# Buffers taken in turn instead of first-free in a one-core attention and mixture kernel

## The chip, the cores and the metric

The kernel runs on one core of a Trainium2 chip. The metric is device time in microseconds (us), the median of several executions. TensorE (PE) does the matmuls; its weight loads have a row of their own (PEld). VectorE (DVE), ScalarE (ACT) and GpSimd (POOL) do the elementwise work, SyncE (SP) issues the transfers. Each engine works through its own list of instructions in order, and waits on semaphores for the others. PSUM, into which the matmuls write, has eight banks of 128 partitions by 512 float32 values.

## The reference, cut to what matters

Two layers follow each other. In the first, each of 4 x 8 heads has 768 queries and keys of 64 values; a query attends only to keys in the same of 64 buckets, which the signs of six projections give. The second is a mixture of 4 causal attention experts over the 512 joined values, of which each position takes the best two.

```python
q_bits = (np.einsum('bhsd,dk->bhsk', q, proj) > 0)          # k_bits alike
mask = q_bucket[:, :, :, None] == k_bucket[:, :, None, :]
scores = np.where(mask, scale * np.matmul(q, k.transpose(0, 1, 3, 2)), -1e9)
x = softmax(scores) @ v                                      # per head, then joined to (B, S, 512)
...
logits = x @ w_gate                                          # the best 2 of 4 experts, softmax weights
for e in range(E):
    scores = np.where(causal, -1e9, scale * (x @ wq[e]) @ (x @ wk[e]).transpose(0, 2, 1))
    out += weight_of(e) * (softmax(scores) @ (x @ wv[e]) @ wo[e])
```

## The kernel before

The program first records its operations, then issues them in a fixed order that is stored in the file (`ORDER`). For each operation the stored order also says on which engine it runs, where two were offered. `Recorder.issue` walks through that order. When an operation touches a tile for the first time, `issue` allocates it from its pool under its name, with `bufs` buffers for that name (`c.pool.tile(...)`), and then calls the engine's method. That call is line 183, and so nearly all instructions of the profile carry line 183; they are told apart by the tiles that they write and read. The order of the instructions on every engine is the order of this list.

The work is a pipeline over units: 32 units "L" (a head of the first layer) and 16 units "M" (an expert of the second, for one batch). Each unit takes these steps, and the steps of several units run beside each other:

- Preparation. For the first layer `prep_pair` does two heads at once. Four times it has ScalarE scale a window of q or k into a PSUM bank named `mx` (`mx<-natq,cs`, `mx<-natk,cs`), copies that to float16 (`qk<-mx` on ScalarE or VectorE) and has VectorE subtract the copy to get the low half (`qk<-mx,qk`). Then 12 small matmuls into `misc` give the bucket signs (`misc<-qk,pbh`). For experts `proj_steps` makes the `qk` tiles from matmuls into `misc`.
- Row maxima. `max_steps` does matmuls into banks named `mx` (`mx<-qk`), and VectorE reduces each to maxima (`pm<-mx`, or `scrap<-mx,causal` in the masked form). `shift_steps` turns the maxima round through `misc` into a row (`negh`, `row`, `fr`) that is added to the queries by a transfer.
- Scores. `s_unit` does matmuls into banks named `st` (`st<-qk`). ScalarE takes the exponential twice, in float32 (`p<-st`) and float16 (`ph<-st`), and GpSimd subtracts (`pl<-p,ph`), so that the attention weights stand in two float16 halves.
- Values. Three matmuls for each 128 keys go into the bank `o` (`o<-vh,ph`, `o<-vl,ph`, `o<-vh,pl`), four or five chunks behind the scores; VectorE divides by the sum (`xp<-o,rden`, `yn<-o,rden`).

The eight PSUM banks are shared out by name: `misc` has two, `o` one, `mx` two, `st` three. The two `mx` banks so serve the ScalarE windows of `prep_pair` and the max matmuls of `max_steps` together:

```python
w = psum.tile([128, 512], FT, name="mx", bufs=2)[:, 0:HS]       # prep_pair
nc.scalar.activation(w, x, AF.Copy, scale=cn)
nc.copy(a[:, ev], w)
marks["t"] = nc.vector.tensor_tensor(r, w, a[:, ev], op=OP.subtract)
...
p = psum.tile([128, 512], FT, name="mx", bufs=2)                # max_steps
nc.tensor.matmul(p[:, o:o + w], d["qa"][0:kr, qs], d["ka"][0:kr, k0:k1], start=True, stop=True)
```

Of the names in SBUF with several buffers, `qk` has 12, `xt` 8, `ph` 7, `pl` 5, `p32` 4, `xp` and `xs` 3, and `fr`, `row`, `rden`, `ot`, `yn`, `wst`, the loads `natq`, `natk`, `natv` and some small ones 2. Where a tile takes a buffer that another tile had, its first operation waits until all operations on the earlier tile are done. In the kernel before, the allocation itself picks the buffer: of the buffers of a name, the one that was given up first, as the program's build reckons it.

Of the kernel before, what the change touches and what calls it, by code (L numbers as in the profile page):

```python
# [115 lines left out]
class Recorder:  # L116
# [56 lines left out]
    def issue(self):  # L173
        def real(x):
            if not isinstance(x, View):
                return x
            return x.real()

        for o, (e, m, args, kw) in self.schedule():
            for c in o.new:  # L180
                if c.real is None:
                    c.real = c.pool.tile(c.shape, c.dtype, name=c.name, bufs=c.bufs)
            getattr(getattr(self.nc, e), m)(*[real(x) for x in args], **{k: real(x) for k, x in kw.items()})  # L183


# [1280 lines left out]
```

## Time and profile before

| | us |
|---|---|
| median of 3 runs | 612.49 (612.16 to 612.70) |
| profiled execution | 612.32 |
| its span, first to last instruction | 610.5 |
| TensorE busy | 591.4 |
| VectorE busy | 524.0 |
| ScalarE busy | 516.8 |
| GpSimd busy | 471.5 |

The granted clock of TensorE was 1.000 of full speed. The busy time of an engine is the part of the span that its instructions cover; matmuls overlap each other, and their ends are modelled, so a TensorE that is busy is not one at its peak. In a timeline an instruction has its start, its duration, its operation as out<-in, and in square brackets how long its engine had been idle and what released it.

### The profile page before, as it was taken

Reading aid. Unit: us, or ns where it says so; the run is one execution under the profiler, and the core shown is the slowest. Engines: PE = TensorE matmul, PEld = TensorE weight load, DVE = VectorE, ACT = ScalarE, POOL = GpSimd, SP = SyncE. Lnnn points to the kernel's source line nnn. Section 1 sums busy time; section 2 is a strip of 40 time slices with the busy share of each in tenths; the row PEclk is TensorE's granted clock in tenths of the full one; section 3 lists DMA queues with packets and bytes.
Section 4 is the critical chain, followed back from the end, with each engine's and each line's share of the span. In section 5 each row is a group of like instructions: output and inputs, shape, how many; then the busy total and the mean of one; then the engine's idle time right before and its main releaser. Section 6 shows DMA issues by size and latency. Waiting matters only on the chain.

```text
span 610.5 us, 20339 instructions
## 1 busy us (share of the span) xinstructions
PE 591.4 (97%) x7754; PEld 432.8 (71%) x7754; DVE 524.0 (86%) x1440; ACT 516.8 (85%) x1132; POOL 471.5 (77%) x540
## 2 busy tenths in 40 slices
PE   8999999999999999999999999999899999999996
PEld 4788887777676767776667676777666677767663
DVE  6999999898899999888989998978988978557973
ACT  7989999999889899958869999987977988934774
POOL 8899989977687889768777888976856888942661
PEclk9999999999999999999999999999999999999999
DMA  6666352231512122331333143222222121001322
GB/s 188 169 189 195 81 146 68 56 99 48 153 40 58 41 87 61 102 104 32 92 89 87 37 119 101 58 83 73 68 87 75 45 48 42 16 21 28 87 79 104
DMA packets 36313, 51.22 MB, mean 84 GB/s; under 512 B 8212, under 2 KB 26104, under 8 KB 36216
## 3 DMA queue, kind: packets, MB, share of 16 engines
q1 hardware_dynamic: 36056, 49.93, 29.7%
q8 instruction: 61, 1.00, 0.7%
q14 instruction: 36, 0.29, 0.2%
q10 hardware_dynamic: 160, 0.00, 0.0%
HBM read 20.98 MB, written 6.29 MB: 45 GB/s over the span
## 4 chain that ended last, share of the span: by engine, by line
PE 67%; DVE 17%; ACT 8%; issue 3%; POOL 2%; DMA 2%; SPq 1%; DVEq 0%; ACTq 0%; POOLq 0%
PE misc L183 22%; PE st L183 19%; PE o L183 16%; PE mx L183 10%; DVE pm L183 6%; ACT p L183 3%; ACT ph L183 3%; DVE qk L183 2%; DVE xt L183 1%; DVE misc L183 1%; POOL pl L183 1%; DVE pmw L183 1%; DMA natq<-in_q_dram 1%; SPq L183 1%; ACT xt L183 1%
## 5 line engine op out<-in xcount | busy, mean ns | idle before, releaser
L183 POOL TENSOR_TENSOR pl<-p,ph 128x512 f16<-128x512 f32 x370 | 409.4, 1126 | 111.3 <-ACT p L183 32.4
L183 PE MATMUL st<-qk 128*128 128x512 f16 (+12 forms) x928 | 229.7, 325 | 2.1 <-ACT p L183 1.0
L183 ACT ACTIVATE ph<-st 128x512 f16<-128x512 f32 x372 | 214.0, 609 | 15.2 <-PE st L183 11.1
L183 ACT ACTIVATE p<-st 128x512 f32<-128x512 f32 x372 | 215.9, 609 | 11.7 <-PE st L183 8.9
L183 PEld LDWEIGHTS <-ph 128*128 128x128 f16 x2880 | 168.1, 98 | 35.5 <-issue 6.5
L183 DVE TENSOR_REDUCE pm<-mx 128x2 f32<-128x512 f32 (+1 forms) x248 | 162.9, 673 | 11.2 <-PE mx L183 8.3
L183 PEld LDWEIGHTS <-pl 128*128 128x128 f16 x1440 | 133.3, 97 | 16.8 <-issue 4.1
L183 PEld LDWEIGHTS <-qk 128*128 128x128 f16 (+4 forms) x1248 | 109.1, 98 | 46.9 <-issue 9.2
L183 PE MATMUL mx<-qk 76*128 76x512 f16 (+2 forms) x464 | 134.3, 326 | 7.2 <-DVE qk L183 4.5
L183 PE MATMUL o<-vh,ph 128*128 128x65 f16 (+1 forms) x1104 | 138.8, 194 | 0.3 <-DVE xp L183 0.3
L183 PE MATMUL o<-vh,pl 128*128 128x65 f16 (+1 forms) x1104 | 138.8, 193 | 0.3 <-POOL pl L183 0.3
L183 PE MATMUL o<-vl,ph 128*128 128x64 f16 x1104 | 138.1, 192 | 0.0
L183 PE MATMUL misc<-xt,wqk_h 128*128 128x384 f16 x256 | 58.6, 325 | 0.0
L183 DVE CUSTOM_DVE_ANT_0 scrap<-mx,causal 128x512 bf16<-128x512 f32 (+2 forms) x96 | 44.4, 462 | 8.8 <-PE mx L183 7.0
L183 DVE TENSOR_REDUCE pmw<-mx 128x2 f32<-128x512 f32 x68 | 44.9, 681 | 2.3 <-PE mx L183 2.0
L183 PE MATMUL o<-mvh,pl 128*128 128x65 f16 x336 | 40.6, 193 | 0.6 <-DVE yn L183 0.6
L183 PE MATMUL o<-mvl,ph 128*128 128x64 f16 x336 | 40.9, 192 | 0.0
L183 PE MATMUL o<-mvh,ph 128*128 128x65 f16 x336 | 40.6, 193 | 0.1
L183 POOL TENSOR_TENSOR vl<-vf,vh 128x384 f16<-128x384 f32 x32 | 29.5, 928 | 11.1 <-PE misc L183 5.1
L183 PEld LDWEIGHTS <-xt 128*128 128x128 f16 x324 | 29.6, 97 | 10.7 <-issue 1.8
L183 PEld LDWEIGHTS <-wqk_h 128*128 128x128 f16 x256 | 24.0, 97 | 14.5 <-issue 1.6
L183 PE MATMUL misc<-wvg_h,xt 128*128 128x260 f16 x192 | 32.1, 274 | 0.7 <-ACT row L183 0.7
(226 smaller groups left out, 1001.2 us busy)
## 6 DMA issues: line engine op xcount, KB each, us to landing
qk<-qk SPq DMA_DIRECT2D x128, 96.0 KB
natv<-in_v_dram SPq DMA_DIRECT2D x16, 384.0 KB
natq<-in_q_dram SPq DMA_DIRECT2D x15, 384.0 KB
natk<-in_k_dram SPq DMA_DIRECT2D x15, 384.0 KB
out_dram<-ot SPq DMA_DIRECT2D x20, 256.0 KB
qk<-qk SPq DMA_DIRECT2D x96, 48.0 KB
qk<-qk SPq DMA_DIRECT2D x8, 192.0 KB
qk<-M SPq DMA_DIRECT2D x48, 24.0 KB
```

What stands on the lines that cost most here:

```text
L183: getattr(getattr(self.nc, e), m)(*[real(x) for x in args], **{k: real(x) for k, x in kw.items()})
```

## The change

A counter is kept for each pool and name. A tile of a name with several buffers is now allocated under that name with a number behind it, which goes round from 0 to `bufs` - 1, and each of these numbered names has a single buffer. So the buffers of a name are used in turn, in the order in which the operations are issued. The list of operations, the engines on which they run and the number of buffers of each name stay as they are.

```diff
+        turn = {}
         for o, (e, m, args, kw) in self.schedule():
             for c in o.new:
                 if c.real is None:
-                    c.real = c.pool.tile(c.shape, c.dtype, name=c.name, bufs=c.bufs)
+                    k = turn[c.pool, c.name] = turn.get((c.pool, c.name), -1) + 1
+                    c.real = c.pool.tile(c.shape, c.dtype, name=f"{c.name}{k % c.bufs}" if c.bufs > 1 else c.name, bufs=1)
             getattr(getattr(self.nc, e), m)(*[real(x) for x in args], **{k: real(x) for k, x in kw.items()})
```

## Rows read from the trace of the kernel before

**Rows 1.** The page: busy time of TensorE, and the chain's shares by engine.
```profile
PE 591.4 (97%) x7754; PEld 432.8 (71%) x7754; DVE 524.0 (86%) x1440; ACT 516.8 (85%) x1132; POOL 471.5 (77%) x540
...
PE 67%; DVE 17%; ACT 8%; issue 3%; POOL 2%; DMA 2%; SPq 1%; DVEq 0%; ACTq 0%; POOLq 0%
```

**Rows 2.** Waits over the span: who waited for whom, us, times, longest.
```profile
DVE pm L183 <- PE mx L183: 8.3, 14, 1.7
...
PE mx L183 <- DVE qk L183: 4.5, 10, 0.9
...
PE st L183 <- ACT p L183: 1.0, 2, 0.6
...
PE st L183 <- ACT ph L183: 0.5, 2, 0.3
```

**Rows 3.** Busy time of each engine by stretch (first column: the stretch).
```profile
core 0: us, PE busy (x) PEld busy (x) DVE busy (x) ACT busy (x) POOL busy (x), PEclk, DMA share, GB/s
108.00:115.00 7.00, 6.83 (x88) 5.33 (x86) 5.12 (x18) 7.00 (x16) 7.00 (x7) 1.00 0.05 10
...
220.00:223.00 3.00, 2.74 (x31) 1.77 (x28) 2.90 (x10) 3.00 (x8) 2.31 (x2) 1.00 0.21 49
288.00:298.00 10.00, 9.01 (x137) 6.40 (x135) 9.42 (x29) 10.00 (x23) 8.56 (x10) 1.00 0.24 71
...
298.00:364.00 66.00, 65.70 (x872) 45.43 (x870) 60.39 (x161) 56.64 (x125) 50.83 (x49) 1.00 0.31 86
...
396.00:402.00 6.00, 5.40 (x61) 4.22 (x58) 4.62 (x17) 5.97 (x15) 3.33 (x4) 1.00 0.06 15
433.00:443.00 10.00, 7.91 (x130) 5.66 (x129) 8.59 (x28) 8.94 (x21) 8.40 (x9) 1.00 0.13 33
```

**Rows 4.** Timeline of TensorE, 435 to 442 us.
```profile
435.25 0.38 PE L183 MATMUL mx<-qk 65*128 65x512 f16 x1 [0.48 <-DVE qk L183]
...
435.83 0.19 PE L183 MATMUL o<-mvh,ph 128*128 128x65 f16 x1
435.86 0.19 PE L183 MATMUL o<-mvl,ph 128*128 128x64 f16 x1
...
438.18 0.39 PE L183 MATMUL mx<-qk 65*128 65x512 f16 x1 [0.91 <-DVE qk L183]
...
441.25 0.27 PE L183 MATMUL mx<-qk 65*128 65x256 f16 x1 [0.70 <-DVE qk L183]
```

**Rows 5.** Timeline of ScalarE, 437 to 440 us.
```profile
437.31 0.27 ACT L183 ACTIVATE fr<-misc 12x128 f16<-12x128 f32 x1 [0.37 <-PE misc L183]
...
438.73 0.56 ACT L183 ACTIVATE mx<-natk,cs 128x384 f32<-128x384 f32 x1
439.96 0.60 ACT L183 ACTIVATE ph<-st 128x512 f16<-128x512 f32 x1 [0.67 <-PE st L183]
```

**Rows 6.** Timeline of VectorE, 435 to 439 us.
```profile
435.78 0.69 DVE L183 CUSTOM_DVE_ANT_0 scrap<-mx,causal 128x512 bf16<-128x512 f32 x1 [0.31 <-PE mx L183]
...
437.58 0.55 DVE L183 TENSOR_TENSOR qk<-mx,qk 128x384 f16<-128x384 f32 x1
438.61 0.69 DVE L183 TENSOR_REDUCE pm<-mx 128x1 f32<-128x512 f32 x1 [0.48 <-PE mx L183]
```

**Rows 7.** Timelines of ScalarE (windows) and VectorE (subtractions) at three other places.
```profile
146.14 0.66 ACT L183 ACTIVATE mx<-natk,cs 128x384 f32<-128x384 f32 x1
...
296.19 0.67 ACT L183 ACTIVATE mx<-natk,cs 128x384 f32<-128x384 f32 x1
...
366.53 0.72 ACT L183 ACTIVATE mx<-natk,cs 128x384 f32<-128x384 f32 x1
...
145.91 0.55 DVE L183 TENSOR_TENSOR qk<-mx,qk 128x384 f16<-128x384 f32 x1
...
296.15 0.56 DVE L183 TENSOR_TENSOR qk<-mx,qk 128x384 f16<-128x384 f32 x1
...
365.89 0.54 DVE L183 TENSOR_TENSOR qk<-mx,qk 128x384 f16<-128x384 f32 x1
```

## The prediction

> **What bounds the kernel now.** I read the busy shares and the chain that ended last first. TensorE is busy 97% of the span, and 67% of the chain is its own work; VectorE holds 17% of it, ScalarE 8% [rows 1]. So time is won only where TensorE stands still, or where VectorE or ScalarE stands on the chain. Second, the waits. TensorE waits for nothing much: the largest entry that buffers can explain is "PE mx <- DVE qk", 4.5 us in 10 waits [rows 2]. A matmul that writes a fresh `mx` bank waits until a VectorE subtraction that writes `qk` is done. No data goes that way: the max matmul reads `qk` tiles of another unit, and what the subtraction does with an `mx` bank is to read and free it. It is a wait for a buffer, which is exactly what the change deals with. Third, the stretches in which these waits lie [rows 3]: 2.1 of the 4.5 us fall into 433 to 443 us (0.48, 0.91 and 0.70, [rows 4]), the rest, 2.4 us, in seven single waits of 0.2 to 0.6 us in 108 to 115, 144 to 148, 188 to 194, 220 to 223, 288 to 298, 364 to 370 and 396 to 402 us. They are the places where `prep_pair` runs beside the max matmuls of a mixture unit.
>
> Look at one of them. At 438.18 the max matmul starts, 0.05 us after the subtraction of 437.58 (0.55 us long) ends, having stood 0.91 us [rows 4, 6]. There are two `mx` banks. The other was given up by the `scrap<-mx` operation that began at 435.78 and took 0.69 us, so at 436.47 [rows 6]. It then lay idle until ScalarE wrote the next `prep_pair` window into it at 438.73 [rows 5]. The bank that was free went to the engine that came late, and the engine that came early was sent to the bank in use.
>
> **What the change does, part by part.** It adds no instruction, removes none and reorders none. Each tile gets buffer number (its count modulo the number of buffers), so it waits for the tile that many places before it in the list of operations, where before it waited for the one whose buffer the allocation had listed as free first. I followed that list for each name. For `p32`, `ph`, `pl`, `pf`, `row`, `rden`, `xp`, the `nat` tiles, `wst`, `yth`, `ytl` and `yn` the tiles are given up in the order in which they are taken, so nothing changes. Another predecessor comes to 50 of 432 `mx` tiles in PSUM, 60 of 240 `misc`, 6 of 393 `st`, 69 of 96 `qk`, 6 of 30 `xt`, 4 of 20 `ot` and 2 of 31 `fr`. Mostly two neighbours in the list swap buffers.
>
> *Removed: the `mx` waits behind `prep_pair`.* In the list the ScalarE window of `prep_pair` stands just ahead of the max matmul, so in turn the window gets the bank of the subtraction and the matmul the bank that is free. In the example the matmul's new predecessor is done at 436.47, 1.71 us before the matmul starts [rows 4, 6]; all ten places are of this kind. The gross gain is the 4.5 us of rows 2. It can be more: a matmul's end is modelled, and 65-column matmuls of 0.19 us start every 0.03 us [rows 4], so each idle time may be up to 0.16 us longer than shown. Ten of these make 1.6, and the upper bound is 6.1 us.
>
> How much is kept? In 433 to 443 us ScalarE is busy 8.94 of 10.00 us and VectorE 8.59, so neither is full [rows 3], and both stand still because of these waits: VectorE 0.31 and 0.48 us for the max matmul itself [rows 6], ScalarE 0.67 us for the next `st` matmul, and 0.37 us for a `misc` one [rows 5]. ScalarE's two make 1.04, which is the least that this stretch gives back; 2.1 is the most. I take 1.5. Elsewhere ScalarE is full: 7.00 of 7, 3.00 of 3, 10.00 of 10, 5.97 of 6 us [rows 3]. There TensorE gets ahead, and whether the lead lasts hangs on what it meets next. After such a stretch TensorE is the pacer again (65.70 of 66 us busy, ScalarE 56.64), and it has to wait for an `st` bank only 1.0 and 0.5 us in the whole run [rows 2, 3], so some lead can be carried out. Between nothing and 2.4 us I take the middle and a little, 1.3.
>
> *Added: the ScalarE window waits for the subtraction.* In most places ScalarE comes to it later than the subtraction ends: at 366.53 the window starts 0.10 us after the subtraction of 365.89 (0.54 us) [rows 7]. In two it would be clearly late: at 296.19 its new predecessor ends at 296.15 + 0.56 = 296.71, 0.52 us later, and at 146.14 it ends at 145.91 + 0.55 = 146.46, 0.32 us later [rows 7]. What stands behind the window on ScalarE are the exponentials of the attention unit, for which GpSimd and then the value matmuls wait. If ScalarE passes all of it on it costs 0.84 us; nothing, if the subtraction itself moves up by what VectorE no longer waits. I take 0.4.
>
> *`misc`, `st`, `xt`, `qk`, `ot`, `fr`.* These swaps I cost at nothing. `misc`, `st` and `xt` swap neighbours both of which are long free, or late by less than 0.2 us. `qk` has 12 buffers and its predecessors are units that ended tens of microseconds before. What hides a single late `qk` tile near 112 us is VectorE's idle time, busy 5.12 of 7.00 us [rows 3]; uncovered it costs at most one VectorE operation of 0.55 us.
>
> *The sum:* 1.5 + 1.3 - 0.4 = 2.4 us. The profiled execution took 612.32 us with a span of 610.5, and lies 0.17 us under the median of 612.49. So 612.32 - 2.4 = 609.9 for that execution and 610.1 for the median.
>
> **Rivals.** *ScalarE holds the gain (no change).* Outside 433 to 443 us ScalarE is full wherever TensorE waits [rows 3], so the lead of TensorE is used up at the next exponential, and in 433 to 443 us only ScalarE's 1.04 us comes back, less the 0.84 us of late windows: 0.2 us, 612.3. For it speak the rows with 10.00 of 10; against it that TensorE hardly ever waits for an `st` bank [rows 2], and that ScalarE is not full after the stretches. The Trainium skill says the same in general: "Perfetto Trace Analysis", section "Identifying the Most-Contended Engine", has the engine with the highest occupancy be the one to improve, and warns that matmul busy time doesn't tell how near TensorE is to its limit. By that rule the 97% of TensorE prove nothing, ScalarE is the engine that counts in these stretches, and the time stays where it is; the trace agrees within the stretches, and not between them.
>
> *All of it is kept.* If TensorE paces everything, 4.5 us go and the hidden parts with them, up to 6.1, with no cost: 606.2 to 607.8 us.
>
> *Slower: ScalarE stalls on VectorE.* Each of some 16 windows now has to wait for a subtraction that VectorE does in its own order. The margin at 366.53 is 0.10 us [rows 7]; if VectorE comes later than ScalarE there by half a subtraction, 0.27 us, each time, ScalarE loses 16 x 0.27 = 4.3 us in stretches where it is full. The point from which this decides is where the loss is above the lead kept, 1.3 / 16 = 0.08 us a window. With 1.3 us kept the time would be 612.3 + 4.3 - 1.3 = 615.3 us. Against it: VectorE also stops waiting for TensorE (8.3 us of "DVE pm <- PE mx", [rows 2]) and comes earlier, not later.
>
> That the change does nothing at all I leave out: the idle bank at 436.47 shows that the old choice is not the turn.
>
> **How the numbers follow.** About 0.2%, 1.2 us, is what a measurement of this kernel can tell from no change. My forecast, a gain of 1.2 to 4 us: 0.53. All kept, above 4 us: 0.12. ScalarE holds it, within 1.2 us of before: 0.24. Slower: 0.11. Faster is then 0.65, same 0.24, slower 0.11. The range goes from 607.0, most but not all of the 4.5 to 6.1 us kept, to 612.8, nothing gained and a part of the late windows paid; the likeliest case alone is 608.5 to 611.3.
>
> **What would show it.** In the changed profile "PE mx <- DVE qk" should be nearly gone, from 4.5 us to under 1. "DVE pm <- PE mx" should be smaller. In 430 to 445 us ScalarE's idle times ahead of `ph` and `fr` should shrink, and the max matmul should start directly behind the matmul before it. A new wait of ScalarE's `mx` window on "DVE qk" should show at a few places, some tenths each. I am wrong if waits on ScalarE or for `st` banks grow by as much as the `mx` waits shrink, or if "ACT mx <- DVE qk" is above 2 us. The counts of instructions on each engine must stay.

## The result, and the profile after

The changed kernel takes 607.04 us (median of 4 runs, 606.84 to 607.49), the kernel before 612.43 us (4 runs, 612.16 to 612.70): ratio 0.9913, 95% interval 0.9896 to 0.9930. The gain is 5.4 us; the forecast was 2.4, with 610.1 us. The profiled execution took 607.13 us, with a span of 605.3. So the direction came as forecast, the time lies 0.04 us inside the low end of the range, and the gain is a little over twice the size.

The page after, answering to [rows 1]: the span, the busy times, and the chain's shares by engine.

```profile
span 605.3 us, 20342 instructions
...
PE 590.1 (97%) x7754; PEld 432.6 (71%) x7754; DVE 523.7 (87%) x1440; ACT 516.7 (85%) x1132; POOL 471.4 (78%) x540
...
PE 78%; ACT 8%; DVE 8%; POOL 2%; issue 2%; DMA 2%; SPq 0%; DVEq 0%; ACTq 0%; POOLq 0%
```

The counts are those of before and no engine has less to do. VectorE's share of the chain has fallen from 17% to 8%, TensorE's has risen from 67% to 78%. That is some 55 us of the chain (104 to 48 us), ten times the gain: the chain now runs over other instructions, and its shares tell where to look, not how much was won. What is gone is told by the waits.

The waits after, answering to [rows 2] (us in total, times, longest):

```profile
ACT ph L185 <- PE st L185: 9.2, 14, 2.2
...
DVE pm L185 <- PE mx L185: 7.7, 14, 1.7
...
PE mx L185 <- DVE pm L185: 2.5, 6, 0.8
...
PE st L185 <- ACT p L185: 1.2, 3, 0.7
...
PE st L185 <- ACT ph L185: 0.5, 2, 0.3
...
ACT mx L185 <- DVE qk L185: 0.2, 1, 0.2
```

"PE mx <- DVE qk", 4.5 us in 10 waits before, has no entry any more. "PE mx <- DVE pm" (2.3 us in 5 waits before) is another wait for an `mx` bank and stays. The wait that the change was to add, ScalarE's window for the subtraction, shows once, with 0.2 us.

The busy times, answering to [rows 3]. The lead is the time by which the changed kernel is ahead; the stretches start about that much earlier, so each starts at about the same work and, where TensorE is faster, covers more of it:

```profile
core 0: us, PE busy (x) PEld busy (x) DVE busy (x) ACT busy (x) POOL busy (x), PEclk, DMA share, GB/s
108.00:115.00 7.00, 7.00 (x90) 5.52 (x90) 5.17 (x18) 7.00 (x16) 7.00 (x8) 1.00 0.04 10
...
286.50:296.50 10.00, 9.52 (x139) 6.50 (x137) 9.54 (x31) 9.93 (x23) 8.53 (x9) 1.00 0.25 72
393.50:399.50 6.00, 6.00 (x74) 4.70 (x71) 5.25 (x18) 5.97 (x15) 3.44 (x4) 1.00 0.06 13
430.00:440.00 10.00, 9.99 (x161) 7.30 (x159) 9.65 (x30) 9.71 (x23) 8.94 (x9) 1.00 0.17 50
```

In the last stretch TensorE is busy 9.99 us of 10 in place of 7.91, and does 161 matmuls in place of 130; VectorE and ScalarE do more there as well. In 393.5 to 399.5 us (396 to 402 before) ScalarE was as full before as it is now (5.97 of 6), and still TensorE went from 5.40 to 6.00.

TensorE in 430 to 437 us, the three max matmuls of [rows 4] and the one ahead of them:

```profile
430.40 0.38 PE L185 MATMUL mx<-qk,qk 76*128 76x512 f16 x1
...
431.75 0.38 PE L185 MATMUL mx<-qk,qk 65*128 65x512 f16 x1
...
433.61 0.38 PE L185 MATMUL mx<-qk,qk 65*128 65x512 f16 x1
...
436.10 0.27 PE L185 MATMUL mx<-qk,qk 65*128 65x256 f16 x1
```

None stands idle now. TensorE does its 7,754 matmuls in the same order in both traces, so each can be put beside itself. The one ahead, and one behind the stretch, in the kernel before:

```profile
433.26 0.38 PE L183 MATMUL mx<-qk 76*128 76x512 f16 x1
...
450.06 0.32 PE L183 MATMUL misc<-xt,wqk_h 128*128 128x384 f16 x1
```

and the one behind it in the changed kernel:

```profile
444.92 0.32 PE L185 MATMUL misc<-xt,wqk_h 128*128 128x384 f16 x1
```

At the one ahead (433.26 and 430.40) the lead is 2.86 us; at the three that follow (435.25, 438.18, 441.25, [rows 4]) it is 3.50, 4.57 and 5.15, and at the one behind still 5.14. The stretch gave 2.3 us.

ScalarE and VectorE there, answering to [rows 5] and [rows 6]:

```profile
434.11 0.27 ACT L185 ACTIVATE fr<-misc 12x128 f16<-12x128 f32 x1
...
435.53 0.56 ACT L185 ACTIVATE mx<-natk,cs 128x384 f32<-128x384 f32 x1
436.03 0.57 ACT L185 ACTIVATE ph<-st 128x512 f16<-128x512 f32 x1
```

```profile
432.44 0.69 DVE L185 CUSTOM_DVE_ANT_0 scrap<-mx,causal 128x512 bf16<-128x512 f32 x1
...
434.24 0.55 DVE L185 TENSOR_TENSOR qk<-mx,qk 128x384 f16<-128x384 f32 x1
434.70 0.68 DVE L185 TENSOR_REDUCE pm<-mx 128x1 f32<-128x512 f32 x1
```

The idle times in brackets of before (0.37 and 0.67 us on ScalarE, 0.31 and 0.48 on VectorE) are gone. The `mx` window of 435.53 starts 0.74 us after its new predecessor, the subtraction of 434.24, has ended: it pays nothing for the turn.

**Where the gain of a full ScalarE comes from.** At 146 us ScalarE has no idle time before the window. ScalarE before, and the first idle times after two other full stretches:

```profile
145.66 0.66 ACT L183 ACTIVATE p<-st 128x512 f32<-128x512 f32 x1
...
146.83 0.49 ACT L183 ACTIVATE qk<-mx 128x384 f16<-128x384 f32 x1
...
147.72 0.28 ACT L183 ACTIVATE xs<-xw,rw 128x1 f32<-128x1 f32 x1
148.98 0.38 ACT L183 ACTIVATE mvh<-misc 128x256 f16<-128x256 f32 x1 [0.98 <-PE misc L183]
...
197.51 0.60 ACT L183 ACTIVATE ph<-st 128x512 f16<-128x512 f32 x1 [0.74 <-PE st L183]
...
302.18 0.60 ACT L183 ACTIVATE p<-st 128x512 f32<-128x512 f32 x1 [1.60 <-PE st L183]
```

ScalarE after, the same instructions and the window of 146.14 of [rows 7]:

```profile
145.38 0.66 ACT L185 ACTIVATE p<-st 128x512 f32<-128x512 f32 x1
146.21 0.59 ACT L185 ACTIVATE mx<-natk,cs 128x384 f32<-128x384 f32 x1 [0.17 <-DVE qk L185]
146.83 0.49 ACT L185 ACTIVATE qk<-mx 128x384 f16<-128x384 f32 x1
...
147.72 0.28 ACT L185 ACTIVATE xs<-xw,rw 128x1 f32<-128x1 f32 x1
148.21 0.38 ACT L185 ACTIVATE mvh<-misc 128x256 f16<-128x256 f32 x1 [0.20 <-PE misc L185]
...
196.39 0.60 ACT L185 ACTIVATE ph<-st 128x512 f16<-128x512 f32 x1 [0.32 <-PE st L185]
...
300.21 0.60 ACT L185 ACTIVATE p<-st 128x512 f32<-128x512 f32 x1 [0.89 <-PE st L185]
```

Read the starts in pairs. At `p` ScalarE is 0.28 us ahead of before; the window waits for the subtraction, and at 146.83 and 147.72 the two traces stand at the very same time: within the stretch ScalarE gained nothing, it lost the 0.28. Then, out of work, it waits for a `misc` matmul, 0.98 us before and 0.20 now, and at `mvh` it is 0.77 us ahead. TensorE had its lead already (at the max matmul that started at 146.51 before it grew by 0.49 us), and ScalarE collected it out of idle time that it no longer has. The waits at 197.51 and 302.18 shrank in the same way, by 0.42 and 0.71 us. Behind three of the other full stretches ScalarE waited 0.17, 0.35 and 0.34 us for TensorE in the kernel before (at 115.75, 371.48 and 404.20) and does not wait there with the change; behind the seventh, 220 to 223 us, the wait is too short for the view.

### The profile page after: what moved, and what is told of

It reads as the page before. It is cut to its first block, busy times and chain, and to the rows that moved or that the text cites. A ratio compares the mean times of both kernels' runs of the same rounds, so it can differ in the third digit from the quotient of the medians.

```text
span 605.3 us, 20342 instructions
## 1 busy us (share of the span) xinstructions
PE 590.1 (97%) x7754; PEld 432.6 (71%) x7754; DVE 523.7 (87%) x1440; ACT 516.7 (85%) x1132; POOL 471.4 (78%) x540
## 4 chain that ended last, share of the span: by engine, by line
PE 78%; ACT 8%; DVE 8%; POOL 2%; issue 2%; DMA 2%; SPq 0%; DVEq 0%; ACTq 0%; POOLq 0%
PE misc L185 24%; PE st L185 24%; PE o L185 19%; PE mx L185 12%; ACT p L185 3%; ACT ph L185 2%; DVE pm L185 2%; POOL pl L185 1%; DVE pmw L185 1%; ACT xt L185 1%; DVE xt L185 1%; DMA qk<-M 1%; DVE qk L185 1%; DMA pbe<-in_proj_dram 0%; DVE scrap L185 0%
## 5 line engine op out<-in xcount | busy, mean ns | idle before, releaser
L185 PE MATMUL st<-qk,qk 128*128 128x512 f16 (+12 forms) x928 | 229.8, 325 | 2.3 <-ACT p L185 1.2
L185 PE MATMUL mx<-qk,qk 76*128 76x512 f16 (+2 forms) x464 | 134.3, 326 | 2.8 <-DVE pm L185 2.5
```

## The experiments

The expectations name theories by letters. A is the prediction's mechanism with "All of it is kept": two `mx` banks, TensorE paces. B and C put the gain elsewhere, in the other names or in the names and places of the buffers as such. D is the rival "ScalarE holds the gain": outside 433 to 443 us nothing can come. E, formed after the first runs, and its rival F are about ScalarE's idle time after the full stretches. All medians are of 5 runs or more; each kernel is compared with the kernel before on its own chip. The changed kernel's 607.04 is from another chip than the runs that are set against it below; the kernel before took 612.43 us on the one and 612.52 on the other, so this adds about 0.1 us of doubt.

**Only the two `mx` banks in turn** (in the kernel before):

```diff
-                    c.real = c.pool.tile(c.shape, c.dtype, name=c.name, bufs=c.bufs)
+                    if c.name == "mx" and c.space == 1:
+                        k = turn[c.name] = turn.get(c.name, -1) + 1
+                        c.real = c.pool.tile(c.shape, c.dtype, name=f"{c.name}{k % c.bufs}", bufs=1)
+                    else:
+                        c.real = c.pool.tile(c.shape, c.dtype, name=c.name, bufs=c.bufs)
```

> Only the two mx banks in PSUM go in turn; all other names keep the choice of the kernel before. Theory A (the gain is TensorE's wait for an mx bank behind the prep_pair subtraction, and TensorE carries the lead to the end): 606.8 to 607.4 us, PE mx <- DVE qk gone. Rival B (the swaps of misc, st, qk and xt bring it): 612.4. Rival C (numbered names change places in memory and waits, whatever the turn): between the two, 609 to 611.

Measured 607.28 us against 612.67: 0.9914, interval 0.9901 to 0.9928. That is the whole gain. Its waits of TensorE have no "PE mx <- DVE qk" either.

**Everything but `mx` in turn:** the same edit with this condition.

```diff
-                    if c.name == "mx" and c.space == 1:
+                    if c.bufs > 1 and not (c.name == "mx" and c.space == 1):
```

> Every name with several buffers goes in turn except the mx banks. Theory A: 612.2 to 612.9 us (the swaps of misc and st cost some tenths here and there and give 0.25 back at one), PE mx <- DVE qk stays at 4.5 us. Rival B: 607. Rival C: 609 to 611.

Measured 612.62 against 612.67: 1.0003, interval 0.9994 to 1.0012. Nothing; the swaps of `misc`, `qk`, `st`, `xt`, `ot` and `fr` are worth nothing that can be measured here (the interval reaches from 0.4 us faster to 0.7 us slower). The wait of TensorE stands:

```profile
PE mx L188 <- DVE qk L188: 4.8, 11, 0.9
```

**Numbered `mx` names, but each tile in its old bank.** SWAPS has the 25 tiles at which the old choice left the turn (it and the next one take each other's place: the 50 tiles of the prediction). The edit is shown against the run with `mx` alone in turn.

```diff
+        SWAPS = (45, 55, 85, 87, 116, 145, 147, 173, 227, 229, 231, 248, 285, 287, 313, 315, 324, 326, 339, 341, 343, 345, 356, 385, 390)
-                        c.real = c.pool.tile(c.shape, c.dtype, name=f"{c.name}{k % c.bufs}", bufs=1)
+                        c.real = c.pool.tile(c.shape, c.dtype, name=f"{c.name}{(k + sum(j <= k for j in SWAPS)) % 2}", bufs=1)
```

> The mx banks have numbered names with one buffer each, but each tile gets the bank that the kernel before gave it. Theory A: 612.2 to 612.7 us, the same as before. Rival C: 607 to 610, since names and places are those of the mx banks in turn.

Measured 612.32 against 612.67: 1.0001, interval 0.9992 to 1.0010 (the medians differ by less than the runs scatter). So it is which bank a tile gets, not the name.

**Only the three pairs of 433 to 443 us in turn:** 339, 341 and 343 taken out of SWAPS.

> As the one with the old choice, but the three pairs of prep_pair window and max matmul between 433 and 443 us are swapped. Theory A: TensorE's three waits there were 0.65, 1.07 and 0.86 us from start to start; less some 0.3 given back that is 2.3, so 610.1 us, and the same lead at the last instruction as at 445 us. Rival D (ScalarE holds the gain wherever it is full, so that this stretch alone, where it has idle time, gives the whole gain of the change): 607.1 to 607.6 us.

Measured 610.31 against 612.67: 0.9966, interval 0.9953 to 0.9978, a gain of 2.4 us. TensorE still waits elsewhere:

```profile
PE mx L189 <- DVE qk L189: 2.4, 7, 0.6
```

**All pairs in turn but these three:** SWAPS = (339, 341, 343).

> The two mx banks go in turn except for the three pairs of window and max matmul between 433 and 443 us, which keep the old choice; all other names as before. So only the stretches in which ScalarE is full can give anything. Theory A (TensorE carries its lead through a full ScalarE): the run with all mx pairs gained 5.4 us, the one with the last three alone 2.4, so 3.0 us here, 609.6. Rival D (a full ScalarE takes the lead back): 612.0 to 612.6.

Measured 609.49 against 612.52: 0.9953, interval 0.9940 to 0.9967, a gain of 3.0 us (2.0 to 3.7 by the interval), all from stretches where ScalarE is full or nearly so (3.97 of 4 us, 5.94 of 6 and 5.98 of 6 in the three that [rows 3] doesn't show).

```profile
PE mx L189 <- DVE qk L189: 2.1, 3, 0.9
```

The two parts make 2.4 + 3.0 = 5.4 us, the whole gain of the change; and the waits that are left in the one (2.4) and in the other (2.1) make the 4.5 of before. The time gained is more than the wait removed in both. D falls: it has nothing for the full stretches, and they gave 3.0 us.

**More work for ScalarE in the changed kernel:** at 16 places the `mx` window is written twice, so about 8 us more (a window and the operation behind it start 0.50 us apart, at 435.53 and 436.03).

```diff
+        TWICE = (85, 87, 116, 145, 147, 173, 227, 229, 231, 285, 287, 313, 315, 339, 341, 343)
...
+            extra = 0
...
+                    if c.name == "mx" and c.space == 1 and k in TWICE:
+                        extra = 1
-            getattr(getattr(self.nc, e), m)(*[real(x) for x in args], **{k: real(x) for k, x in kw.items()})
+            for _ in range(1 + extra):
+                getattr(getattr(self.nc, e), m)(*[real(x) for x in args], **{k: real(x) for k, x in kw.items()})
```

> The changed kernel, with ScalarE writing 16 of its mx windows twice, those in the stretches where the mx waits were (the same values, so the result stays). A window takes some 0.5 us from start to start, so ScalarE gets 8 us more work there. Theory A: TensorE paces even there, and ScalarE's later windows reach it only where the subtraction of a window is needed at once: 607 to 610 us. Rival D: ScalarE sets the time where it is full: 613 to 615.

Measured 615.18, 8.1 us above the changed kernel's 607.04 (against the kernel before 1.0041, interval 1.0027 to 1.0055). The page and the waits of TensorE:

```profile
PE 594.7 (97%) x7754; PEld 433.1 (71%) x7754; DVE 524.0 (85%) x1440; ACT 525.4 (86%) x1148; POOL 471.9 (77%) x540
```

```profile
PE st L190 <- ACT p L190: 3.0, 8, 0.6
...
PE st L190 <- ACT ph L190: 1.9, 5, 0.5
```

ScalarE is busy 8.7 us longer, and 8.1 of it shows at the end. TensorE now waits for ScalarE to give up `st` banks, 4.9 us in place of 1.7. That TensorE alone paces, which A needs, is not so.

**More work for TensorE in the changed kernel:** the first max matmul behind each of these 16 windows is issued three times in a row (TWICE one higher each, `extra = 2`).

> The changed kernel, with TensorE doing the first max matmul behind each of those 16 windows three times (it starts afresh each time, so the result stays): 10 of 512 columns at 0.215 us and 6 of 256 at 0.108, twice more, 5.6 us of TensorE work. Theory A: all of it is added, 612.2 to 612.8 us. Rival D: TensorE has time to spare in these stretches: 607 to 609.

Measured 611.08, 4.0 us above 607.04 (against the kernel before 0.9976, interval 0.9967 to 0.9985).

```profile
PE 595.1 (98%) x7786; PEld 435.6 (71%) x7786; DVE 523.7 (86%) x1440; ACT 517.0 (85%) x1132; POOL 471.5 (77%) x540
```

TensorE is busy 5.0 us longer by the page, and 4.0 of it reach the end. From start to start in the two traces each of the 16 places puts TensorE back by 0.43 us (512 columns) or 0.22 (256), 5.6 us together; a part comes back further on, at 292.54 and 344.74 of the changed trace, where TensorE had waited for an exponential and for a transfer and, coming later, no longer waits (0.33 and 0.34 us). So both engines are on the path in these places.

This asked for a theory that has both: **E**, ScalarE has a backlog in the full stretches, and in the kernel before it made up for it in the idle time that it had behind them because TensorE came late. The change spent that idle time: TensorE's lead lasts because ScalarE, ready to wait there anyhow, meets it. Then ScalarE's work must be cheaper in the kernel before than in the changed one. F: ScalarE sets the pace in these stretches in both kernels. Two runs, the same doublings in the kernel before:

> The kernel before, with ScalarE writing the same 16 mx windows twice (the same values). On the changed kernel this cost 8.1 us, all of the work added. Theory E (ScalarE's backlog in the full stretches is worked off in the idle time that TensorE's waits left it afterwards; the change used up that idle time): the cost is smaller here, by about the 5 us of waits, 3 to 6 us, 615.5 to 618.5. Rival F (ScalarE sets the pace in these stretches in both kernels): 8 us again, 620.5.

Measured 616.62 against 612.82: 1.0063, interval 1.0050 to 1.0077, 3.8 us more.

```profile
PE 593.2 (96%) x7754; PEld 433.2 (70%) x7754; DVE 524.8 (85%) x1440; ACT 525.8 (86%) x1148; POOL 471.8 (77%) x540
```

```profile
PE mx L189 <- DVE qk L189: 5.6, 10, 1.2
...
PE st L189 <- ACT ph L189: 1.4, 4, 0.5
PE st L189 <- ACT p L189: 1.3, 3, 0.6
```

ScalarE is busy 9.0 us longer, and only 3.8 reach the end; with the change 8.1 of 8.7 did. The waits for `st` banks are 2.7 us, not 4.9. That is what E expects, and F's 8 us is missed.

E speaks of the full stretches, but a part of the difference comes from 433 to 443 us, where ScalarE was not full. Three of the 16 windows lie there. The same two matmuls around it as above, with the doubled windows in the changed kernel and in the kernel before:

```profile
437.09 0.38 PE L190 MATMUL mx<-qk,qk 76*128 76x512 f16 x1
...
453.20 0.32 PE L190 MATMUL misc<-xt,wqk_h 128*128 128x384 f16 x1
```

```profile
437.67 0.38 PE L189 MATMUL mx<-qk 76*128 76x512 f16 x1
...
454.64 0.32 PE L189 MATMUL misc<-xt,wqk_h 128*128 128x384 f16 x1
```

From one to the other TensorE took 14.52 us with the change and takes 16.11 with the doubled windows, 1.6 more; before it took 16.80 and takes 16.97, 0.2 more. There the idle time that hid the work lay inside the stretch (ScalarE busy 8.94 of 10 us before). The 13 windows in the full stretches, some 6.5 us of work, put TensorE back by 6.5 us with the change and by 4.2 before, read in the same way between the matmuls that start at 100 and at 420 us of the trace of before. So ScalarE was near the path there before too, and E's part is about 2.2 of the 3.7 us of difference that this gives. (As a whole the trace with doubled windows is 4.3 us longer than that of before, which is from another chip; the medians on one chip are 3.8 apart.)

> The kernel before, with TensorE doing the first max matmul behind each of the 16 windows three times, 5.6 us of TensorE work; on the changed kernel it cost 4.0. Theory E (TensorE is the pacer of the kernel before also where it waits, since its waits are longer than ScalarE's backlog lasts): 4 to 5.6 us, 616.5 to 618.1. Rival F: ScalarE is full there, and TensorE's extra work is hidden in part: under 3 us, below 615.5.

Measured 616.78 against 612.82: 1.0067, interval 1.0053 to 1.0081, 4.0 us more, as much as in the changed kernel (TensorE busy 597.0 us in place of 591.4). TensorE's work costs the same in both, at the low edge of what E gave; it was on the path in these places before and after. F's number, under 3, is missed.

**A better choice than the turn?** At four pairs the old choice gave the tile that comes first the bank that is free first; there the banks were put back, the rest left in turn.

```diff
+        BACK = {("mx", 1): (248,), ("misc", 1): (102, 132, 162)}
-                    k = turn[c.pool, c.name] = turn.get((c.pool, c.name), -1) + 1
+                    n = turn[c.pool, c.name] = turn.get((c.pool, c.name), -1) + 1
+                    k = n + sum(j <= n for j in BACK.get((c.name, c.space), ()))
```

> The changed kernel, with the old choice put back for the four pairs of buffers in which the turn sent TensorE to the bank that came free later: one mx pair (near 324 us of before) and three misc pairs (283, 346 and 426 us). Theory A: TensorE lost 0.07, 0.07, 0.14 and 0.20 us there and has part of it back soon after, so 0.2 to 0.5 us less than the changed kernel, 606.6 to 606.9. If these swaps cost nothing in the end: 607.0.

Measured 607.15 against 612.52: 0.9916, interval 0.9902 to 0.9929. No different from the change (607.04) or from `mx` alone (607.28); the 606.6 to 606.9 of theory A did not come. Five runs, from 606.92 to 608.30, can't tell it from "these swaps cost nothing"; nothing large is left in these four.

## Why the prediction was right, and what was too small

The direction and the place of the gain were read rightly, the size was not. The likeliest case, 608.5 to 611.3, was missed, and what came is the case "all kept, above 4 us" that was given 0.12. That the range from 607.0 on still holds 607.04 is luck. The rivals' times 606.2 to 607.8 and 615.3 are counted from the profiled 612.3 and the forecast from the median of 612.49; the 0.2 us between them decide nothing here.

**What bounds the kernel** was read rightly: the wait "PE mx <- DVE qk" is a wait for a bank, it is what the change removes, and its banks are all of the gain (`mx` alone 607.28, the rest alone 612.62, the names alone 612.32).

**The gross gain** was bounded too low. The prediction took 4.5 us, at most 6.1, from the idle times. Putting each max matmul beside itself in the two traces, TensorE's lead steps up at 13 places, by 0.20 to 1.07 us, 6.8 us together. The ten places of the view make 6.1 of it, just the prediction's upper bound. Three more, at 294.12, 296.76 and 369.24, where the view has no such wait, make 0.7. At each of the 13 the step is the idle time in the trace plus 0.16 us (at these three 0.15, 0.04 and 0.06 us are idle). At 400.36 it can be seen. TensorE before, the max matmul and the matmul ahead of it:

```profile
399.57 0.19 PE L183 MATMUL o<-mvh,ph 128*128 128x65 f16 x1
400.36 0.38 PE L183 MATMUL mx<-qk 65*128 65x256 f16 x2 [0.60 <-DVE qk L183]
```

and after:

```profile
397.36 0.19 PE L185 MATMUL o<-mvh,ph 128*128 128x65 f16 x1
397.39 0.38 PE L185 MATMUL mx<-qk,qk 65*128 65x256 f16 x2
```

From start to start it is 0.79 us before and 0.03 after: 0.76 us lost, where the view has 0.60. The prediction had seen that the modelled end hides up to 0.16 us at each wait, and left that in the upper bound where it belonged in the sum.

**"How much is kept?" is the step that failed, in its sizes.** For 433 to 443 us it took 1.5 us (1.04 to 2.1); the three pairs alone gave 2.4. For the other stretches it took 1.3 us between 0 and 2.4, half given back because ScalarE is full; they gave 3.0. The noise of each part (1.3 to 2.9 and 2.0 to 3.7 by their intervals) reaches below these upper ends, but the sum, 5.4 us with 4.3 to 6.4, is far from 2.4. The reason that it gave for keeping some, that TensorE paces behind these stretches and ScalarE is not full there, was right, and should have been followed to its number. Behind the full stretches ScalarE waited 0.98, 0.74 and 1.60 us for TensorE; these rows were there to be read in the trace of before, and 0.77, 0.42 and 0.71 us of them are what came back, 1.9 us at three places.

**The late windows (-0.4 us)** are real on ScalarE and cost the end nothing that shows. At 146.14 ScalarE lost 0.35 us from `p` to the window (0.28 ahead, then 0.07 behind; 0.32 was forecast); at 296.19 its window runs 1.17 us ahead where the `p` in front of it ran 1.49 ahead, 0.32 lost (0.52 was forecast). But the loss fell in front of idle time, as in the rows of 146 to 148 us and at 302.18, where ScalarE had 1.60 us to spare.

**The swaps at nothing** are right (1.0003).

**The rivals.** "All of it is kept" (606.2 to 607.8) gave the time, 607.04, though not by its own road: TensorE does not pace everything, as the doubled windows show (8.1 us more), and of the 6.8 us some are given back. Steps down of TensorE's lead by 0.1 us or more make 2.4 us together, other steps up of that size 1.5, and with the smaller ones 5.5 us are left at the last matmul. Two of the largest steps down, 0.33 and 0.34 us, are where the changed kernel waits for an exponential (at 292.54, 294.44 before) and for a `qk` transfer (at 344.74, 346.37 before); no run was made to try what takes the lead back. "ScalarE holds the gain" falls: its place, the full stretches, gave 3.0 us. The Trainium skill's rule that went with it ("Perfetto Trace Analysis", section "Identifying the Most-Contended Engine": the engine with the highest occupancy is the one to improve) does not decide here by the occupancy of a stretch: at 396 to 402 us ScalarE was busy 5.97 of 6 us before [rows 3], TensorE's lead grew by 0.76 us at 400.36, and the full stretches together moved the end by 3.0 us. "Slower" falls: "ACT mx <- DVE qk" is 0.2 us, where it needed some 16 waits of 0.27.

**What would show it** came as written: the max matmuls start behind the matmul before them, `ph` and `fr` lose their idle time, "DVE pm <- PE mx" goes from 8.3 to 7.7 us, the `st` waits from 1.5 to 1.7.

Open is how far a choice by true release times could go in all names; four pairs gave nothing.

## What to carry to other kernels

When one name's buffers serve two engines that run apart in time, "the buffer that was listed as free first" can send the early engine to a buffer that is still in use while the other lies idle. Look for a wait on an engine from which no data comes, and then for the other buffer's last user; the order in which buffers are given out can be worth 0.9% with no buffer, instruction or order changed. To size what such a wait is worth when another engine is full in the same stretch, look at that engine's next idle time and what ends it: if it is the engine that was held up, the lead can be collected there, as it was behind the full stretches of this kernel.

## What was not expected of the hardware

The idle times of TensorE in a trace fell short of what the engine lost, by a third: 4.5 us in 10 waits against 6.8 us in 13 steps from start to start. At each of the 13 the shown idle time is 0.16 us too short, which is just what a 65-column matmul is shown longer than the next one's start allows (0.19 us long where the next starts 0.03 us later); three of the waits were so short that the view had none. And the same 16 doubled windows of ScalarE, about 0.5 us each, cost 3.8 us in one order of banks and 8.1 us in the other: ScalarE's busy share of the whole run, 85% in both kernels, does not tell this price. It went with the idle time that ScalarE had near the work: behind the stretch where it was full, inside the stretch at 433 to 443 us.
